# An adaLN block with dilated local attention and an MLP: two token streams in paired 64-row tiles, with Q, K and V on column tiles of the raw weights

## The chip, the cores and the metric

The kernel runs on one core of a Trainium2 chip. The metric is device time in microseconds (us) of one launch. A core has a matrix engine (TensorE, PE in the profile; its weight loads are listed as PEld), a vector engine (VectorE, DVE), an activation engine (ScalarE, ACT), a general engine (GpSimd, POOL), and a queue of its own for transfers (SyncE, SP). Each engine works through its own list of instructions in order and waits on semaphores for the others. Matmuls write into PSUM, which has eight banks; DVE and ACT read it out ("evacuate" it). TensorE's array of 128 x 128 can be used as smaller tiles: a "64x128" matmul uses 64 of its rows, and two of these, on row tiles 0 and 64, can stand in the array together; "128x32" uses 32 of its columns, and so on. Here this is called the tile mode.

## The reference

One block over 2048 tokens of width 448: a modulated layer norm, attention in which each token sees itself and seven tokens before it at a distance of 2, 4, ... 14, an output projection, a second modulated norm followed by a third norm inside the MLP, and an MLP of width 1792. Inputs and outputs are bf16.

```python
def _A_ref(x, wqkv, wo):
    B, S, D = x.shape
    H = 16
    Dh = D // H
    W, dil = (8, 2)
    qkv = (lambda x, *d: x.transpose(*d))((x @ wqkv).reshape(B, S, 3, H, Dh), 2, 0, 3, 1, 4)
    ...
    logits = jnp.where(mask[None, None, :, :], logits, -1000000000.0)
    attn = _softmax(logits, axis=-1)
    o = jnp.einsum('bhsw,bhswd->bhsd', attn, vg)
    return (lambda x, *d: x.transpose(*d))(o, 0, 2, 1, 3).reshape(B, S, D) @ wo

def _B_ref(x, w1, b1, w2, b2):
    y = _layernorm(x, axis=-1)
    h = _gelu(jnp.einsum('bsd,df->bsf', y, w1) + b1)
    return jnp.einsum('bsf,fd->bsd', h, w2) + b2
...
mod = (_silu(c) @ w_mod).reshape(c.shape[0], 6, 1, -1)
sa, ca, ga, sb, cb, gb = (mod[:, 0].copy(), mod[:, 1].copy(), mod[:, 2].copy(), mod[:, 3].copy(), mod[:, 4].copy(), mod[:, 5].copy())
h = _layernorm(x, axis=-1) * (1 + ca) + sa
x = x + ga * _A_ref(h, A_wqkv, A_wo)
h = _layernorm(x, axis=-1) * (1 + cb) + sb
x = x + gb * _B_ref(h, B_w1, B_b1, B_w2, B_b2)
```

## The kernel before

**Tokens.** With a dilation of 2, even and odd tokens never meet in the attention. So the tokens are split by parity into two streams of 1024, which lie one behind the other on the free axis (`tok_col`). A block is 128 tokens of one stream; there are 16.

**Order.** The program first records every piece of work as a task with an engine, a cost, its readers and writers and its buffers (`Planner.add`). `Planner.plan` then places the tasks in time with these costs, over several turns with noise, and `emit` writes the instructions out in the order of the best plan, with warm-up matmuls (`filler`) where PE would wait in the first 12 us. What each engine runs in which order is thus set by the planner. PSUM is divided into two double buffers (room "L", two banks each) and four single ones (room "S").

**Front.** `front_ln` takes a layer norm of some blocks (statistics L513 and L514, a reciprocal root on ACT or on POOL at L531, normalizing L536), transposes them on PE (L607) and applies the modulation in the evacuation (DVE L581, ACT L585), so that `hT` holds the normed input with the width on partitions, in four passes of 128, 128, 128 and 64 rows. `spread` (L626) copies the Q and K weights into `Wqk`, in which every head of 28 columns has 32. `front_qk` multiplies (L640): eight groups of four heads, four passes each, up to 512 tokens to a matmul, evacuated by ACT (L652) or DVE (L649). `mods` (L661) computes four of the six modulation vectors in 128x32 tiles, sends them through memory to all partitions, and folds two of them into the projection and w2 weights (L676, L685).

**Attention.** It works in nine blocks of two sub-blocks; a sub-block is two windows of 57 queries with 64 keys each. `values` copies the two windows out of `hT` (`hw`, L702) and multiplies them with the V weights (L708). The logits (L733) stand with keys on partitions, in 32x64 tiles; ACT takes the exponential (L743), DVE multiplies with the mask (L751). Then one group of matmuls sums the weights of each head (pd, L765, with a matrix of ones) and one forms the weighted values (po, L773), both in 64x32 tiles with the head's width on partitions. ACT turns the sums into reciprocals with a logarithm and an exponential (L785, L788), and DVE multiplies (L798) into `oT`, again 32 rows to a head.

**Rest.** `out_proj` (L814) projects a block of 128 tokens in four passes, and DVE adds the residual (L818); then come the second and the third norm (L829 to L836), a DMA transpose into `yT` (L840), and on POOL the residual with the MLP's bias (L844). `mlp` takes a tile of 256 tokens: w1 (L864) in 14 groups of 128 columns, four passes each, whose last pass has 64 rows and a row of ones that carries the bias b1; GELU on ACT (L871); w2 (L885) with 14 passes for each of two blocks; DVE adds (L892) and SP stores two blocks at once (L905). Exponentials and GELUs need different function tables on ACT, so the work is divided into four phases (`PHASES`): attention blocks 0 to 2 and MLP tile 0, and so on; w1 of a phase stands behind that phase's logits.

Of the kernel before, what the change touches and what calls it, by code (L numbers as in the profile page):

```python
# [11 lines left out]
FP32 = mybir.dt.float32  # L12
# [5 lines left out]
DP = 512  # L18
KT, KR = 4, 64
KW = (128, 128, 128, KR)  # L20
KE = (128, 128, 128, KR + 1)
HP = 32
FT = F // 128
WIN = 8
SL = 1024
LEAD, SEP = 8, 8
WQ, WK, WE = 57, 64, 58
SBQ, NSB, NBT = 2 * WQ, 18, 9
SBE = 4 * WE
WT = LEAD + SL + SEP + SL + 4  # L30
OTW = NSB * SBQ
NBLK = S // 128
EPS = 1e-5
DEN_SCALE = 2.0 ** -32
EXP_SET = "natural_log_exp_and_others"
START, NOISE, WINDOW = 0.8, 0.02, 3.4133
SEED, TURNS = 44, 60
QKE = "AAADAAAD"
BONUS = (0.0, 0.0, 0.0)
SPREAD = (("DVE", "DVE"), ("DVE", "DVE"))  # L40
PHASES = [
    (range(0, 3), [0]),
    (range(3, 5), [1, 2]),
    (range(5, 7), [3, 4]),
    (range(7, 9), [5, 6, 7]),
]
LMM, DMM = 0.55, 0.80
FILL_UNTIL, FILL_SHARE = 12.0, 1.0
ROOM = {"L": 2, "S": 4, "et": 2, "den": 2, "zh": 6, "yT": 3, "hm": 3, "vb": 4, "hw": 3}
SWITCH, SAME = 0.095, 1.0  # L50
SEM = 0.07
DRAIN = {"PE": 0.165, "DVE": 0.085, "ACT": 0.105, "POOL": 0.05, "SP": 0.0}


class Buf:


    def __init__(self, room, make, name=""):
        self.room, self.make, self.name, self.users, self._t = room, make, name, [], None
        self.slot = None  # L60
# [8 lines left out]
class Task:  # L69
    def __init__(self, n, eng, us, fn, bufs, rank_add, late, dense, port, mode):  # L70
        self.n, self.eng, self.us, self.fn, self.bufs = n, eng, us, fn, bufs
        self.name = f"{eng} {fn.__qualname__.split('.')[-1]}:{fn.__code__.co_firstlineno}"
        self.rank_add, self.late, self.dense, self.port, self.mode = rank_add, late, dense, port, mode
        self.before, self.after = {}, []
        self.rank = 0.0
        self.fill = 0


class Planner:

    def __init__(self):
        self.tasks, self.writer, self.readers = [], {}, {}

    def add(self, eng, us, fn, reads=(), writes=(), bufs=(), after=(), order_after=(), rank_add=0.0, late=0.0, dense=1.0, port=False, mode="F"):
        t = Task(len(self.tasks), eng, us, fn, bufs, rank_add, late, dense, port or eng == "POOL", mode)
        for k in list(reads) + [b for b in bufs]:
            if k in self.writer:
                self._edge(self.writer[k], t, True)  # L90
        for k in writes:
            if k in self.writer:
                self._edge(self.writer[k], t, True)
            for r in self.readers.get(k, ()):
                self._edge(r, t, True)
            self.writer[k], self.readers[k] = t, []
        for k in reads:
            self.readers.setdefault(k, []).append(t)
        for b in bufs:
            b.users.append(t)  # L100
        for a in after:
            self._edge(a, t, True)
        for a in order_after:
            self._edge(a, t, False)
        self.tasks.append(t)
        return t

    def wrote(self, task, *bufs):
        for b in bufs:
            self.writer[b] = task  # L110

    def _edge(self, a, b, full):
        if a is b:
            return
        if a not in b.before:
            a.after.append(b)
            b.before[a] = full
        else:
            b.before[a] = b.before[a] or full

    def ranks(self):
        for t in reversed(self.tasks):
            tail = 0.0
            for a in t.after:
                lag = (DRAIN[t.eng] + SEM + t.late) if a.before[t] else 0.0
                tail = max(tail, a.rank + lag)
            t.rank = t.us + tail + t.rank_add

    def backward(self):

        used = {e: [] for e in DRAIN}
        for t in sorted(self.tasks, key=lambda t: (-(t.start + t.us), -t.n)):
            tail = 0.0
            for a in t.after:
                same = a.eng == t.eng and (t.eng == "PE" or not a.before[t])
                lag = 0.0 if same or not a.before[t] else DRAIN[t.eng] + SEM + t.late
                tail = max(tail, a.rank + lag)
            spans = used[t.eng]
            k = bisect.bisect_left(spans, (tail, 0.0))
            if k > 0 and spans[k - 1][1] > tail:  # L140
                tail = spans[k - 1][1]
            while k < len(spans) and spans[k][0] < tail + t.us - 1e-9:
                tail = max(tail, spans[k][1])
                k += 1
            t.rank = tail + t.us
            spans.insert(k, (tail, t.rank))

    def forward(self):
        left = {t: len(t.before) for t in self.tasks}
        ready_at = {t: 0.0 for t in self.tasks}  # L150
        ready = {e: [] for e in DRAIN}
        for t in self.tasks:
            if left[t] == 0:
                ready[t.eng].append(t)
        room = {r: [0.0] * n for r, n in ROOM.items()}
        users_left = {b: len(b.users) for t in self.tasks for b in t.bufs}
        free_at = {e: START for e in DRAIN}
        order = []
        now = START
        mode = "F"  # L160
        port = {"DVE": 0.0, "POOL": 0.0}
        while len(order) < len(self.tasks):
            started = False
            for e in ("PE", "DVE", "ACT", "POOL", "SP"):
                if free_at[e] > now:
                    continue
                best, best_key = None, None
                shared = e in port and port["DVE" if e == "POOL" else "POOL"] > now
                for t in ready[e]:
                    if ready_at[t] > now or (shared and t.port):  # L170
                        continue
                    key = (t.rank + (SAME if e == "PE" and t.mode == mode else 0.0), -t.n)
                    if best is not None and key < best_key:
                        continue
                    need = {}
                    for b in t.bufs:
                        if b.slot is None:
                            need[b.room] = need.get(b.room, 0) + 1
                    if all(sum(x <= now for x in room[r]) >= n for r, n in need.items()):
                        best, best_key = t, key  # L180
                if best is None:
                    continue
                t = best
                t.fill = 0
                if e == "PE" and now < FILL_UNTIL:
                    t.fill = int(max(0.0, now - free_at[e]) * FILL_SHARE / (0.43 if now < 6.8 else 0.215))
                ready[e].remove(t)
                order.append(t)
                t.start = now
                started = True  # L190
                for b in t.bufs:
                    if b.slot is None:
                        b.slot = min(range(ROOM[b.room]), key=lambda k: room[b.room][k])
                        room[b.room][b.slot] = 1e9
                end = now + t.us
                if e == "PE" and t.mode != mode:
                    end += SWITCH
                    mode = t.mode
                free_at[e] = end
                if t.port:  # L200
                    port[e] = end
                done = end + DRAIN[e] + t.late
                for b in t.bufs:
                    users_left[b] -= 1
                    if users_left[b] == 0:
                        room[b.room][b.slot] = done + SEM
                for a in t.after:
                    left[a] -= 1
                    at = done + SEM if a.before[t] else end
                    if a.eng == e == "PE" or (a.eng == e and not a.before[t]):  # L210
                        at = end
                    ready_at[a] = max(ready_at[a], at)
                    if left[a] == 0:
                        ready[a.eng].append(a)
            if started:
                continue
            times = [v for v in free_at.values() if v > now] + [v for r in room.values() for v in r if now < v < 1e9]
            times += [ready_at[t] for e in ready for t in ready[e] if ready_at[t] > now]
            if not times:
                return None, 1e9  # L220
            now = min(times)
        return order, max(t.start + t.us + t.late for t in self.tasks)

    def clear(self):
        for t in self.tasks:
# [755 lines left out]
```

## Time and profile before

| What | us |
|---|---|
| median of 3 runs (lowest, highest) | 187.85 (187.34, 188.03) |
| span of the profiled execution, first to last instruction (the page has no other time of it) | 184.8 |
| PE busy; w1 (L864), w2 (L885), Q/K (L640) | 173.5; 52.3, 46.9, 30.0 |
| DVE busy | 124.6 |
| ACT busy; GELU (L871), exponentials (L743), denominators (L785, L788) | 103.8; 28.8, 16.0, 8.5 and 9.6 |
| POOL busy | 47.5 |
| first Q/K matmul, first w1 matmul, end of the last w2 matmul | 10.3, 54.0, 180.6 |

A line of the profile's costliest groups names the source line, the engine, the operation, what it writes and reads, the size, and how often it runs; behind the bar stand the busy time of all of them in us, the mean of one in ns, and the time for which the engine stood idle just ahead of them, with the instruction that ended it. Matmuls are pipelined, so the mean of one is longer than the distance to the next. A line of the chain in order of time has the start, the length, the engine, the tile, the line and how many instructions are merged in it; a line of the table of stretches has the stretch, its length, then the busy time and number of instructions of PE, PEld, DVE, ACT and POOL, then the granted TensorE clock as a share of full speed, the share of time in which the DMA engines were busy, and GB/s. The granted clock was 1.000 over the whole span.

### The profile page before, as it was taken

To read this page: it belongs to the slowest core of one execution; us is meant where nothing else is said; L and a number is where in the kernel's file an instruction comes from. 1 tells how busy PE (TensorE), PEld (TensorE's weight loads), DVE (VectorE), ACT (ScalarE), POOL (GpSimd) and SP (SyncE) were. 2 spreads that over 40 slices of the span, in tenths; PEclk is the share of its full clock that TensorE was granted. 3 is DMA by queue.
4 is the path that set the end of the run, shared out by engine and by line. 5 is a ranking of instruction groups with operands and counts; after the bars stand their busy time and mean duration, and the time that the engine had idled before them with its cause. 6 is when DMAs were issued, how large, how long until landed. Compare 5 with 4: busy or idle time off the path is not lost.

```text
span 184.8 us, 5433 instructions
## 1 busy us (share of the span) xinstructions
PE 173.5 (94%) x2325; PEld 111.5 (60%) x2333; DVE 124.6 (67%) x348; ACT 103.8 (56%) x139; POOL 47.5 (26%) x97
## 2 busy tenths in 40 slices
PE   3997789899999999999999999999999999999991
PEld 0574565455458655775855567678556756857750
DVE  3799599889899799688424389693346968711102
ACT  2167667767486877766585667426786530521230
POOL 7074000508501602334200060532001526200000
PEclk9999999999999999999999999999999999999999
DMA  5999779900110101301210100213001012040101
GB/s 172 304 356 265 193 175 313 326 14 7 27 32 0 28 5 32 82 0 28 42 18 0 52 5 4 57 50 48 14 4 53 0 32 78 0 103 7 51 0 50
DMA packets 19004, 13.99 MB, mean 76 GB/s; under 512 B 9246, under 2 KB 18403, under 8 KB 18980
## 3 DMA queue, kind: packets, MB, share of 16 engines
q1 hardware_dynamic: 18978, 13.64, 27.7%
q8 instruction: 18, 0.29, 0.7%
q14 instruction: 6, 0.05, 0.1%
q10 hardware_dynamic: 2, 0.00, 0.0%
HBM read 9.70 MB, written 1.84 MB: 62 GB/s over the span
## 4 chain that ended last, share of the span: by engine, by line
PE 90%; DVE 4%; issue 2%; DMA 1%; ACT 1%; DVEq 0%
PE p L864 27%; PE p L885 23%; PE pq L640 13%; PE pv L708 7%; PE pw L814 7%; PE pwm L506 3%; PE lt L733 3%; PE po L773 3%; PE ptr L607 1%; PE pd L765 1%; DMA yT<-ybuf 1%; DVE st_all L513 1%; DVE kT L649 1%; ACT lden L788 1%; PE pb L661 0%
## 5 line engine op out<-in xcount | busy, mean ns | idle before, releaser
L864 PE MATMUL p<-yT,w_s 128*128 128x256 bf16 x448 | 52.3, 272 | 0.1
L871 ACT ACTIVATE hm<-p 128x1024 bf16<-128x1024 f32 (+1 forms) x32 | 28.8, 916 | 36.8 <-PE p L864 36.8
L864 PEld LDWEIGHTS <-w_s 128*128 128x128 bf16 x448 | 43.3, 97 | 8.9 <-issue 0.6
L885 PE MATMUL p<-w_s,hm 128*128 128x448 bf16 x224 | 46.9, 353 | 0.0
L531 POOL TENSOR_TENSOR rs_all<-tv_all,neg_half 128x1 f32<-128x1 f32 (+1 forms) x35 | 20.9, 605 | 52.3 <-DVE tv_all L528 47.5
L885 PEld LDWEIGHTS <-hm 128*128 128x128 bf16 x224 | 21.2, 98 | 17.9
L844 POOL TENSOR_TENSOR x1p_ring<-x_all,gbb_bc 128x448 f32<-128x448 bf16 x16 | 17.2, 1079 | 54.6 <-DVE x_all L818 45.3
L640 PE MATMUL pq<-hT,Wqk 128*128 128x512 bf16 (+3 forms) x153 | 30.0, 334 | 0.5 <-issue 0.2
L892 DVE TENSOR_TENSOR x_all<-p,x1p_ring 128x448 bf16<-128x448 f32 x16 | 9.8, 618 | 26.0 <-PE p L885 26.0
L640 PEld LDWEIGHTS <-Wqk 128*128 128x128 bf16 (+1 forms) x160 | 15.1, 97 | 11.5 <-DVE Wqk L626 0.2
L513 DVE BATCH_NORM_STATS2 st_all<-x_all 128x6 f32<-128x448 bf16 x32 | 19.1, 617 | 0.7 <-DMA x_all<-in_A_x_dram 0.5
L743 ACT ACTIVATE et<-lt 128x928 bf16<-128x928 f32 x18 | 16.0, 941 | 5.0 <-PE lt L733 4.9
L708 PE MATMUL pv<-Wv,hw 128*128 128x448 bf16 x72 | 16.4, 353 | 1.6 <-DVE hw L702 0.9
L751 DVE TENSOR_TENSOR et<-et,mask 128x928 bf16<-128x928 bf16 x18 | 11.7, 649 | 5.3 <-ACT et L743 5.3
L814 PE MATMUL pw<-wo_s,oT 128*128 128x448 bf16 x64 | 14.4, 352 | 0.0
L712 ACT CAST vbuf<-pv 128x448 bf16<-128x448 f32 x18 | 9.6, 532 | 6.3 <-PE pv L708 6.2
L818 DVE TENSOR_TENSOR x_all<-pw,x_all 128x448 bf16<-128x448 f32 x16 | 9.9, 620 | 4.4 <-PE pw L814 4.2
L785 ACT ACTIVATE lden<-pd 128x928 f32<-128x928 f32 x9 | 8.5, 948 | 7.1 <-PE pd L765 7.1
L652 ACT CAST kT<-pq 128x512 bf16<-128x512 f32 (+1 forms) x14 | 7.1, 510 | 8.6 <-PE pq L640 8.2
L708 PEld LDWEIGHTS <-hw 128*128 128x128 bf16 x72 | 6.7, 97 | 7.7 <-issue 1.2
L798 DVE TENSOR_TENSOR oT<-po,lden 128x456 bf16<-128x456 f32 x18 | 10.6, 623 | 0.6 <-ACT lden L788 0.6
L833 DVE BATCH_NORM_STATS2 st_all<-h 128x6 f32<-128x448 bf16 x16 | 9.8, 621 | 0.1
(83 smaller groups left out, 172.3 us busy)
## 6 DMA issues: line engine op xcount, KB each, us to landing
out_dram<-x_all SPq DMA_DIRECT2D x8, 224.0 KB, 2.0
w_s<-in_B_w_dram SPq DMA_DIRECT2D x2, 784.0 KB, 12.3
wmod<-in_w_mod_dram SPq DMA_DIRECT2D x2, 672.0 KB, 7.5
w_s<-in_B_w_dram SPq DMA_DIRECT2D x1, 1344.0 KB, 9.1
x_all<-in_A_x_dram SPq DMA_DIRECT2D x1, 896.0 KB, 7.9
wm_st<-in_w_mod_dram SPq DMA_DIRECT2D x1, 720.0 KB
wqk_st<-in_A_wqkv_dram SPq DMA_DIRECT2D x2, 339.0 KB, 5.7
x_all<-in_A_x_dram SPq DMA_DIRECT2D x2, 224.0 KB
```

Of the source, the lines that this page charges most:

```text
L513: add("DVE", 0.53, lambda: nc.vector.bn_stats(out=st_all[:, sl, :], in_=src()), reads=key, writes=[f"st{sl}"])
L531: lambda: nc.gpsimd.tensor_tensor(out=rs_all[:, which, b0:b0 + n], in0=tv_all[:, which, b0:b0 + n], in1=neg_half[:, 0:n], op=ALU.pow),
L640: nc.tensor.matmul(pq.t[:], lhsT=wqk_m(kt, m), rhs=hT[0:KE[kt], kt, c0:c0 + n], start=(kt == 0), stop=(kt == KT - 1))
L708: nc.tensor.matmul(pv.t[:], lhsT=hw.t[0:KE[kt], kt].rearrange("p j k -> p (j k)"), rhs=Wv[0:KE[kt], kt, :], start=(kt == 0), stop=(kt == K ...
L743: ex = add("ACT", 0.825, lambda half=half: nc.scalar.activation(out=et.t[:, 2 * half:2 * half + 2].rearrange("p r n ft c -> p r (n ft c)") ...
L751: nc.vector.tensor_tensor(out=ev, in0=ev, in1=mask[:], op=ALU.mult)
L798: nc.vector.tensor_tensor(out=out, in0=pos[j].t[:], in1=rden.t[:, j, :, :, 0:WQ], op=ALU.mult)
L814: nc.tensor.matmul(pw.t[:], lhsT=oT[:, ft, c0:c0 + 128], rhs=wo_s[:, ft, :], start=(ft == 0), stop=(ft == 3))
L844: nc.gpsimd.tensor_tensor(out=x1p_ring[:, t % NX1P, :], in0=x_all[:, t, :], in1=gbb2_bc[:], op=ALU.add)
L864: nc.tensor.matmul(p1.t[:, f // 2, f % 2 * 256:f % 2 * 256 + 256], lhsT=w1_s[0:kp, kt, (fq + f) * 128:(fq + f + 1) * 128], rhs=yT.t[0:kp, ...
L871: gl = add("ACT", 0.18 + nf * 0.183, lambda fq=fq, nf=nf, p1=p1: nc.scalar.activation(out=hm.t[:, fq:fq + nf, :], in_=p1.t[:, 0:nf // 2, : ...
L885: nc.tensor.matmul(p2.t[:], lhsT=hm.t[:, ft, bi * 128:(bi + 1) * 128], rhs=w2_s[:, ft, :], start=(ft == 0), stop=(ft == FT - 1))
```

## The change

The kernel is written anew on the same mathematics.

- **Streams.** The two parities stand side by side: a pair p holds 128 tokens of each stream, and there are eight pairs. x is loaded and stored by pairs, with the two tokens of a row of memory together.
- **w1 and the output projection** contract over seven passes of 64 rows instead of three of 128 and one of 64. Stream 0 lies on partitions 0 to 63 and stream 1 on 64 to 127; each pass is two matmuls in 64x128 mode, one for each stream, which write different banks. The bias b1 moves into the GELU instruction. An MLP tile has 512 tokens (256 of each stream), so there are four tiles instead of eight.
- **Q, K and V** take the weights as they were loaded (`Wqkv`). Q and K: four heads at a time, each in its own 128x32 column tile, 32 raw columns from the head's first (the surplus lands in rows that are not used). V: the windows of 64 keys are read straight from `hT`, in 128x64 tiles.
- **Attention.** One batch of 114 queries of both streams, nine batches. The logits and the mask are as before. V has a 29th column of ones, so that the weighted values come with their denominators. They now stand with queries on partitions (L580, 64x64 tiles, 64 matmuls of 29 columns); DVE takes a reciprocal (L588) and multiplies (L590), and 28 matmuls with the identity (L602, 64x64 tiles) turn the result into the layout of the projection, evacuated by ACT or DVE (L609, L610). The separate sums and ACT's logarithm and exponential of them are gone.
- **PSUM** is four double buffers for everything.
- **Phases.** Three instead of four: batches 0 to 4 and tile 0, batches 5 and 6 and tile 1, batches 7 and 8 and tiles 2 and 3.
- **Loads.** The modulation weights are laid out as 4 x 112 rows, one DMA for each part; the last four pairs of x come ahead of the second part. Half of the projection weights and of w1 is issued from ACT's queue.
- **Order.** The planner is gone; the order of the tasks, the buffers they use, some choices of engine ("53:A" is task 53 on ACT) and three groups of warm-up matmuls (f3, f10, f5, in pairs) are written out as lists (`ORDER`, `SLOTS`). In this order all Q/K, seven of nine V groups, five batches of logits and values and four projections stand ahead of the first w1 matmul on PE.

The core of the diff:

```diff
+UNITS = [[0], [1], [2, 3], [4, 5], [6, 7]]
+PHASES = [(range(0, 5), [0]), (range(5, 7), [1]), (range(7, 9), [2, 3])]
+ROOM = {"P": 4, "et": 2, "os": 2, "den": 2, "z": 3, "h2": 3, "yb": 2, "yT": 2, "hm": 2, "vb": 2, "vf": 1, "xp": 3}
...
+ORDER = """
+0 2 26 9 4 10 33 24 32 11 5 1 3 12 29 13 14 15 28 f3 34 16 17 30 36 35 18 37 19 44 20 27 31 21 38 46 22 23 45 39 47 6
+40 25 7 48 8 49 51 50 f10 41 52 43 42 54 53:A 55 56:A f5 57 65 59 58 67 63 66 60 68 97 69 61 70 99 64 71 72 62 139 98
...
+    def filler(n):
+        for k in range(n):
+            for i in range(2):
+                rows = slice(KS * i, KS * i + KS)
+                nc.tensor.matmul(pwm.t[:, i, 0:512], lhsT=warm_w[rows, 0:128], rhs=warm_w[rows, :],
+                                 start=True, stop=True, tile_position=(KS * i, 0))
...
-            def mm(m=m, pq=pq):
-                for kt in range(KT):
-                    nc.tensor.matmul(pq.t[:], lhsT=wqk_m(kt, m), rhs=hT[0:KE[kt], kt, c0:c0 + n],
-                                     start=(kt == 0), stop=(kt == KT - 1))
+            def mm(m=m, pq=pq):
+                for a in range(2):
+                    for kt in range(KT):
+                        for r in range(4):
+                            w0, w = ((m + a) * 4 + r) * DH, HP if r < 3 else DH
+                            nc.tensor.matmul(pq.t[HP * r:HP * r + w, a, 0:NS * n], lhsT=Wqkv[0:KE[kt], kt, w0:w0 + w],
+                                             rhs=hT[0:KE[kt], NS * kt:NS * kt + NS, c0:c0 + n], start=(kt == 0),
+                                             stop=(kt == KT - 1), tile_position=(0, HP * r))
...
+        def vmm():
+            for kt in range(KT):
+                for j in range(2):
+                    for n in range(NS):
+                        nc.tensor.matmul(pv.t[WK * j:WK * j + WK, n, 0:D],
+                                         lhsT=hT[0:KE[kt], NS * kt + n, kc + WQ * j:kc + WQ * j + WK],
+                                         rhs=Wqkv[0:KE[kt], kt, 2 * D:3 * D], start=(kt == 0), stop=(kt == KT - 1),
+                                         tile_position=(0, WK * j))
...
+        def pmm():
+            for r in range(4):
+                for ft in range(4):
+                    h = 4 * ft + r
+                    for s in range(NS):
+                        for j in range(2):
+                            rows, col = slice(WK * j, WK * j + WK), j if s == 0 else 1 - j
+                            e0 = ((r * 2 + s) * 4 + ft) * WE
+                            nc.tensor.matmul(po.t[WK * col:WK * col + WK, s, HP * h:HP * h + DH + 1],
+                                             lhsT=et.t[rows, e0:e0 + WK], rhs=vb.t[rows, s, h, 0:DH + 1],
+                                             start=True, stop=True, tile_position=(WK * j, WK * col))
...
+        add("DVE", 0.27, lambda: nc.vector.reciprocal(out=rden.t[:], in_=heads()[:, :, :, DH]), bufs=[po, rden], fills=[rden],
+            name="rden")
+        add("DVE", 1.0, lambda: nc.vector.tensor_tensor(
+            out=osb.t[:].rearrange("p s (h e) -> p s h e", h=H), in0=heads()[:, :, :, 0:DH],
+            in1=rden.t[:].unsqueeze(3).to_broadcast([128, NS, H, DH]), op=ALU.mult),
+            bufs=[po, rden, osb], fills=[osb], name="omul")
...
+        def omm():
+            for k in range(KP):
+                for s in range(NS):
+                    for j in range(2):
+                        col = j if s == 0 else 1 - j
+                        rows = slice(WK * col, WK * col + WK)
+                        nc.tensor.matmul(pt.t[KS * s:KS * s + KS, j, k * WQ:k * WQ + WQ],
+                                         lhsT=osb.t[rows, s, k * KS:(k + 1) * KS], rhs=ident[rows, WK * col:WK * col + WQ],
+                                         start=True, stop=True, tile_position=(WK * col, KS * s))
...
-            for ft in range(4):
-                nc.tensor.matmul(pw.t[:], lhsT=oT[:, ft, c0:c0 + 128], rhs=wo_s[:, ft, :],
-                                 start=(ft == 0), stop=(ft == 3))
+            for k in range(KP):
+                for s in range(NS):
+                    rows = slice(KS * s, KS * s + KS)
+                    nc.tensor.matmul(pw.t[:, s, 0:D], lhsT=hT[rows, k, 128 * p:128 * p + 128], rhs=wo_s[rows, k, :],
+                                     start=(k == 0), stop=(k == KP - 1), tile_position=(KS * s, 0))
...
+                    for k in range(KP):
+                        for s in range(NS):
+                            rows = slice(KS * s, KS * s + KS)
+                            nc.tensor.matmul(p1.t[:, s, 256 * fi:256 * fi + 256], lhsT=w1_s[rows, k, f * 128:(f + 1) * 128],
+                                             rhs=yT.t[rows, k, :], start=(k == 0), stop=(k == KP - 1),
+                                             tile_position=(KS * s, 0))
...
+            for fi in range(2):
+                f = 2 * g + fi
+                gelus.append(add("ACT", 0.49, lambda f=f, fi=fi, p1=p1: nc.scalar.activation(
+                    out=hm.t[:, f], in_=p1.t[:, :, 256 * fi:256 * fi + 256], func=ACT.Gelu_apprx_tanh,
+                    bias=b1_col[:, f:f + 1]), reads=["b1"], bufs=[p1, hm], writes=[(hm, f)], after=[tbl], name="gelu"))
```

## The prediction

> **What bounds the kernel now.** I read the page first (busy shares, then the chain that ended last), then the table of stretches, then the chain in order of time. TensorE is the bound: it is busy for 94% of the span, and the chain runs through PE for 90% of it.
>
> ```profile
> PE 173.5 (94%) x2325; PEld 111.5 (60%) x2333; DVE 124.6 (67%) x348; ACT 103.8 (56%) x139; POOL 47.5 (26%) x97
> ...
> L864 PE MATMUL p<-yT,w_s 128*128 128x256 bf16 x448 | 52.3, 272 | 0.1
> ```
>
> L864 is the w1 product: 448 matmuls, with 0.1 us of idle time before all of them. The stretches show where PE waits (column 2 is the length, column 3 PE's busy time):
>
> ```profile
> 10.50:54.00 43.50, 39.17 (x643) 23.12 (x644) 38.94 (x110) 29.96 (x52) 14.02 (x46) 1.00 0.62 171
> 54.00:76.30 22.30, 22.19 (x407) 14.57 (x410) 20.21 (x56) 16.67 (x21) 5.03 (x8) 1.00 0.14 31
> 76.30:180.60 104.30, 104.19 (x1221) 70.21 (x1220) 57.84 (x155) 54.21 (x62) 23.77 (x33) 1.00 0.13 29
> ```
>
> From 54.0 (the first w1) to 180.6 PE never waits; before it, 4.3 of 43.5 us are idle, with DVE as busy as PE. So an instruction taken off PE is worth its spacing after 54, and before 54 the waits decide too. Spacings come from the chain in order of time (start, us, what), since a matmul's mean of 272 ns overlaps its neighbours:
>
> ```profile
> 7.97 0.78 PE ps_col L563 x32
> ...
> 18.23 0.87 PE pb L661 x16
> ...
> 30.69 3.47 PE pq L640 x16
> ...
> 64.25 0.63 PE lt L733 x64
> ...
> 67.64 0.63 PE lt L733 x63
> 68.28 0.86 PE p L885 x4
> ...
> 87.59 6.17 PE p L864 x56
> ...
> 106.28 1.51 PE pw L814 x8
> ...
> 108.55 0.32 PE pd L765 x8
> 108.87 0.55 PE po L773 x64
> ```
>
> Read here: w1 costs 6.17/56 = 0.110 us for 256 columns, the output projection 1.51/8 = 0.189 for 448, Q/K 3.47/16 = 0.217 for 512. Four w2 matmuls take 0.76 elsewhere in the chain but 0.86 behind a logits group in another tile mode, so one mode change costs 0.10. The pd row carries eight matmuls of 464 columns on 2 row tiles by 4 column tiles: one after the other they would take 8 x 0.19 = 1.5 us, and they take 0.32. Tiles of the array do run side by side, in both directions. The pb row says it for 128x32 tiles alone: 16 matmuls of 448 columns in 0.87, four rounds of 0.19 and a mode change.
>
> **The sum, against the span of 184.8.**
>
> *w1 in row pairs.* 448 matmuls become 784, two streams in row tiles 0 and 64, each pair writing two banks, as pd did. At one spacing per pair: 392 x 0.110 = 43.2 instead of 49.4: -6.2. The seventh half-filled contraction pass (64 rows and a bias row) is what disappears. *Output projection:* 64 x 0.189 = 12.1 becomes 56 pairs, 10.6: -1.5. w2 stays at 224.
>
> *Mode changes.* Counting the places where the PE order changes tile mode: 39 before, 60 after, 21 x 0.10 = +2.1.
>
> *Q/K on raw columns.* 160 matmuls become 640 in 128x32 mode, four to a round, 160 rounds of the same columns. Bounds: nothing (pb's 0.87 is 0.76 and one mode change), or the whole surplus of pb, (0.87 - 0.76)/4 = 0.028 a round, +4.4. I take +0.5, near the lower end, because the mode change explains nearly all of it. V, in two 128x64 column tiles, keeps 72 rounds; bounds 0 and 72 x 0.028 = 2.0, taken as 0 on the same row.
>
> *Attention.* Before: pd and po, 0.87 a block, 0.77 without the mode change. After: 64 matmuls in 64x64 tiles and 28 that turn the result back. At po's 0.55/64 = 8.6 ns each, 0.55 + 0.24 = 0.79: +0.2 over nine blocks. At logits' 0.63/64 = 9.8 ns they make 0.90, +1.2. No row has four 64x64 tiles; the far end is a rival below. I take po's price, the nearest shape.
>
> *Start.* Before its 32 column matmuls PE runs 7 warm-up matmuls at 3.07/7 = 0.44 us; the new order puts 10 pairs there, +1.3 if they are as slow. Against it the spreading copies of the Q/K weights go (DVE, 9.90 to 10.78, just ahead of the first Q/K at 10.51), worth up to 0.3. I take +0.7, so Q/K starts at 11.2. The four evacuations of the first unit keep their prices (0.73 for two on DVE, 1.02 for two on ACT).
>
> *End.* Before, two adds (1.15 us together) and a 224 KB store stand behind the last matmul; after, one add (0.62) and half that store: -0.6.
>
> *Other engines.* ACT loses the logarithm and exponential of the denominators (9 x 0.948 + 9 x 1.069 = 18.1) and gains about 4 in smaller GELUs (56 x 0.595 against 24 x 1.024 + 8 x 0.595) and some 4 in evacuations of the turned output. DVE loses 1.8 of spreading and 5.4 of window copies, and its 18 divisions (10.6) become nine of double width (L818's 0.62 for 448 columns gives about 1.1, an estimate: 9.8) with nine reciprocals (some 0.2 each). All counted as nothing: from the first w1 on both have slack (58 and 54 us busy of 104). Without that cover a w2 evacuation of 1.1 us would stop PE eight times, +9.
>
> *Waits.* w1 now stands behind five attention blocks instead of three, all Q/K and seven of nine V groups. PE's work up to there: Q/K 28.4, V 7 x 1.51 = 10.6, logits and values 5 x (0.53 + 0.79) = 6.6, projection 5.3, transposes 3.2 (seven of 0.45), modulation 0.9, 36 mode changes 3.6: 58.6, so w1 could begin at 69.8. DVE's list up to the second y of the first pair, at the spacings of the chain and timeline (statistics 0.53, normalizing 0.31, mask 0.55), comes to 53 us from about 5: it ends 11 us sooner if never held up, where before its slack was 43.5 - 38.9 = 4.6. The wait on window copies (0.9 us of PE idle) goes. I lower idle time, 5.1 before by the same sums, by 1.1. *DMA:* the six-vector modulation weights now come behind 1.2 times the bytes (5.4 against 4.5 MB, which were in by about 18), so near 21.5 at that rate, and part of the projection weights rides on ACT's queue from the start. Their matmuls (L481) stand in PE's order at about 24; were they late, every Q/K behind them would wait, and then the scale rows and the w1 and w2 loads behind those on SP's queue. The DMA transposes go from 16 to 8 with seven blocks instead of four; 2.4 us to landing now, up to 7/4 of it then, behind which only w1 of a later pair stands, with other PE work ahead.
>
> Sum: -6.2 - 1.5 + 2.1 + 0.5 + 0.2 + 0.7 - 0.6 - 1.1 = -5.9, span 178.9. The runs' median, 187.85, is 3.05 above the profiled span; the page gives no other time of that execution, and I keep the difference: **181.9 us**.
>
> **Rivals.**
>
> *1. The 64x64 matmuls take turns (slower).* In po and pt both row tiles write the same bank, on different partitions. Before, pd, po and the logits gave each row tile a bank of its own, so no row shows it. If the two row tiles alternate, 0.79 becomes 1.58 a block, +7.1: 189.0. It decides from +6.9 on (187.85 + 0.5%). For it: the overlap that pd's 0.32 shows is with a bank for each. Against: the partitions differ.
> The Trainium skill (TensorEngine Tiling, Restrictions and Gotchas, Gotcha 1) says that different row tiles can't access one bank at the same time; no run here shows it yet, and by that rule this rival is the result.
>
> *2. Weight loads come into the open in the column tiles.* ps_col is nearly all weight loads: 0.78/32 = 24 ns each. Four a round on 160 rounds, if none were hidden, +15.6: 197.5. Against it: pb, whose 16 loads leave nothing to see.
> The Trainium skill (TensorEngine Tiling, Restrictions) says column tiling switches Fast Weight Load off; pb's 0.87 gives no sign of a cost.
>
> *3. Row pairs don't overlap.* Then w1 is 784 x 0.110 and the projection 112 x 0.189: +53.8, 235.7. pd's 0.32 speaks against it.
>
> *4. The first stage starves.* All products now share four two-bank buffers where two double and four single ones stood, and all engines follow one fixed list. If PE idles as it did from 10.5 to 30 (3.2 of 19.5 us) over all of its 58.6 us, that is 11.6 instead of 4.0: +7.6, 189.5; half of it 185.7. For it: DVE was as busy as PE there. Against: DVE's slack of 11 us.
>
> **How the numbers follow.** Forecast 0.68 (own range 177 to 186), rival 1 0.11, rival 2 0.06, rival 3 0.03, rival 4 0.12. The lower end, 176.5, is the forecast with Q/K at nothing (-0.5), the start at its other bound (-1.0) and none of the 4.0 us of idle time left; the upper, 190, takes in rivals 1 and 4; rivals 2 and 3 and scraps, about a tenth, are left out. About 0.5% is what runs of this kernel can tell from no change (their spread is 0.4%): 186.9 to 188.8. Faster: 0.66 of the forecast and 0.02 of rival 4. Same: 0.02 of the forecast, 0.02 of rival 1 (half paid), 0.03 of rival 4. Slower: the rest, 0.25.
>
> **What would show it.** 28 w1 matmuls (one group of L675) in 1.54 us of chain; the projection's 14 in 1.33; 32 Q/K of 512 in 1.74; L580 0.55 and L602 0.24 a block (twice that is rival 1); first Q/K near 11.2, first w1 near 74; no PE idle time behind it. A first w1 beyond 80, or PE waiting for DVE after it, would make the prediction wrong.

## The result and the profile after

The changed kernel is slower: 198.03 us (median of 4 runs, 196.81 to 199.34) against 187.94 for the kernel before on the same chip, a ratio of 1.0575 with a 95% interval of 1.0471 to 1.0679. The forecast was 181.9 with a range of 176.5 to 190.0, so it was wrong in direction and in range. The profiled execution took 196.81 us, with a span of 195.0 (forecast: 178.9). Of most of these programs some executions are a few per cent slower, at a lower granted clock; the ratios below compare the others, and the traces of e1 and e10 come from such slow executions.

The page of the changed kernel, the same rows as before: the engines' busy time, the w1 group, then the granted clock in the 40 slices and two rows on DMA.

```profile
PE 173.0 (89%) x3463; PEld 111.0 (57%) x3463; DVE 117.7 (60%) x272; ACT 93.7 (48%) x128; POOL 40.1 (21%) x71
...
PEclk9999879998569999999999999999999999999998
...
q8 instruction: 27, 0.44, 1.0%
...
HBM read 11.70 MB, written 1.84 MB: 69 GB/s over the span
...
L675 PE MATMUL p<-yT,w_s 64*128 64x256 bf16 x784 | 44.3, 269 | 0.4 <-issue 0.4
```

TensorE is as long busy as before (173.0 against 173.5), and w1 runs almost without idle time, as forecast. But PE's share fell from 94% to 89%, and the clock drops twice, around 25 and around 52 us. The queue q8 brings instructions: 27 pieces of 16 KB, where the page before has these rows:

```profile
q8 instruction: 18, 0.29, 0.7%
...
HBM read 9.70 MB, written 1.84 MB: 62 GB/s over the span
```

The stretches say where the time is. First the two parts that the first w1 matmul (89.58) divides, then the first part in six pieces; columns as in the table before (PE's busy time is the third, the clock the one after the last engine, then the DMA share).

```profile
9.92:89.58 79.66, 63.17 (x1665) 38.20 (x1667) 55.20 (x129) 39.31 (x50) 12.95 (x16) 0.91 0.48 129
89.58:191.69 102.11, 101.38 (x1720) 69.16 (x1716) 57.09 (x126) 51.83 (x73) 22.07 (x24) 1.00 0.13 33
```

```profile
10.00:23.00 13.00, 8.77 (x269) 6.97 (x270) 9.75 (x31) 7.37 (x13) 1.48 (x2) 1.00 1.06 306
23.00:26.50 3.50, 3.49 (x55) 2.65 (x56) 2.17 (x8) 1.12 (x2) 0.00 (x0) 0.51 0.44 91
26.50:43.00 16.50, 14.68 (x441) 9.00 (x439) 11.58 (x26) 8.83 (x12) 3.72 (x5) 1.00 0.49 114
43.00:47.00 4.00, 2.79 (x144) 1.97 (x141) 3.55 (x9) 3.01 (x5) 0.00 (x0) 1.00 1.06 375
47.00:57.20 10.20, 4.26 (x40) 2.32 (x43) 2.69 (x4) 3.29 (x5) 0.00 (x0) 0.50 0.76 195
57.20:89.58 32.38, 29.10 (x728) 15.21 (x722) 25.37 (x54) 15.69 (x17) 7.75 (x9) 1.00 0.09 17
```

The second part is as forecast: 102.1 us, where the sum had 101.5 (178.9, less 73.8 for the first w1 and 3.6 for the tail). The whole miss lies before the first w1, which came at 89.6 instead of 73.8. PE was idle there for 16.5 us instead of 4.0, and from 47.0 to 57.2 it worked for 4.26 us in 10.2, at half clock, while DVE was busy for only 2.7 us, ACT for 3.3 and POOL not at all. The chain in order of time shows what it waited for (start, length, what; "issue" is a wait with no releaser):

```profile
19.80 1.48 PE pq L458 x36
21.28 1.73 issue
23.01 2.92 PE pq L458 x51
...
44.27 0.23 PE po L580 x8
44.50 1.21 issue
45.72 0.62 PE po L580 x56
46.34 0.63 PE lt L553 x60
46.97 0.92 PE ptr L428 x8
47.89 5.94 issue
53.83 1.03 PE ptr L428 x8
54.87 3.02 PE pq L458 x28
57.89 0.61 PE po L580 x64
...
76.41 1.84 PE pq L458 x32
...
82.58 0.57 PE pt L602 x56
...
89.58 10.70 PE p L675 x196
...
149.19 1.32 PE pw L622 x14
```

The first two cut a group of like matmuls in two: in the list of PE's instructions the first falls 13 matmuls into a group of 32, after one matmul of a round of four, and the second between 8 and 56 of 64 weighted values. No data can be missing there. The third stands between the transposes of two pairs; the second pair's input had been normalized on VectorE at 45.0, 2.9 us before the wait began. What fails to come is the instructions themselves. Counting TensorE's rows in the trace (weight loads, matmuls, semaphores) from its first, the three waits begin after 705, 1729 and 1985 rows, each of them 193 + 256 k. The two waits without releaser in the trace before are at rows 449 and 961, the same series, and they too split a group:

```profile
19.41 0.12 PE po L773 x18
19.53 1.29 issue
20.82 0.49 PE po L773 x42
...
34.47 0.52 PE po L773 x61
35.00 0.70 issue
35.70 0.20 PE po L773 x3
```

So PE's program arrives in pieces of 256 instructions, by the DMA engines, and PE stands where a piece ends and the next has not landed.

### The profile page after: what moved, and what is told of

It is laid out like the page before. It is cut to its first block, busy times and chain, and to the rows that moved or that the text cites. A ratio compares the mean times of both kernels' runs of the same rounds, so it can differ in the third digit from the quotient of the medians.

```text
span 195.0 us, 7547 instructions
## 1 busy us (share of the span) xinstructions
PE 173.0 (89%) x3463; PEld 111.0 (57%) x3463; DVE 117.7 (60%) x272; ACT 93.7 (48%) x128; POOL 40.1 (21%) x71
## 3 DMA queue, kind: packets, MB, share of 16 engines
HBM read 11.70 MB, written 1.84 MB: 69 GB/s over the span
## 4 chain that ended last, share of the span: by engine, by line
PE 74%; DMA 10%; issue 5%; DVE 4%; ACT 4%; ACTq 0%; DVEq 0%
PE p L694 22%; PE p L675 21%; PE pq L458 10%; PE pv L531 8%; PE pw L622 6%; DMA wo_s<-in_A_wo_dram 4%; DMA Wqkv<-in_A_wqkv_dram 3%; PE po L580 3%; DMA mod_bc<-mod_hbm 3%; DVE hT L610 2%; PE lt L553 2%; ACT hT L439 2%; DVE wo_s L495 1%; ACT hT L609 1%; PE pt L602 1%
## 5 line engine op out<-in xcount | busy, mean ns | idle before, releaser
L683 ACT ACTIVATE hm<-p,b_col 128x512 bf16<-128x512 f32 x56 | 35.6, 684 | 31.0 <-PE p L675 30.8
L675 PE MATMUL p<-yT,w_s 64*128 64x256 bf16 x784 | 44.3, 269 | 0.4 <-issue 0.4
L675 PEld LDWEIGHTS <-w_s 64*128 64x128 bf16 x784 | 37.8, 94 | 6.3 <-issue 1.0
L458 PE MATMUL pq<-hT,Wqkv 128*32 128x512 bf16 (+7 forms) x640 | 32.7, 357 | 4.0 <-ACT hT L439 2.1
L399 POOL TENSOR_TENSOR rs_all<-tv_all,neg_half 128x2 f32<-128x2 f32 x22 | 17.0, 782 | 87.4 <-DVE tv_all L397 84.5
L458 PEld LDWEIGHTS <-Wqkv 128*32 128x32 bf16 (+3 forms) x640 | 17.9, 101 | 16.5 <-issue 7.0
L383 DVE BATCH_NORM_STATS2 stt<-x_all 128x6 f32<-128x448 bf16 x32 | 18.6, 609 | 1.8 <-DMA x_all<-in_A_x_dram 1.7
L659 POOL TENSOR_TENSOR Wqkv<-x_all,gbb_bc 128x448 f32<-128x448 bf16 x12 | 12.9, 1097 | 32.6 <-DVE x_all L704 17.7
L531 PE MATMUL pv<-Wqkv,hT 128*64 128x448 bf16 (+1 forms) x144 | 15.3, 359 | 2.2 <-DMA Wqkv<-in_A_wqkv_dram 1.1
L622 PE MATMUL pw<-wo_s,hT 64*128 64x448 bf16 x112 | 11.6, 350 | 3.6 <-ACT hT L609 2.3
```

What stands on the lines that cost most here:

```text
L383: add("DVE", 0.53, lambda: nc.vector.bn_stats(out=stt[:, w, b, :], in_=src()), reads=reads, bufs=bufs, writes=[f"st{w}_{b}"], name="stats")
L399: add("POOL", 0.42 + 0.15 * n, lambda: nc.gpsimd.tensor_tensor(out=r, in0=tv, in1=neg_half[:, 0:n], op=ALU.pow), reads=[f"tv{w}_{b0}", "ne ...
L458: nc.tensor.matmul(pq.t[HP * r:HP * r + w, a, 0:NS * n], lhsT=Wqkv[0:KE[kt], kt, w0:w0 + w], rhs=hT[0:KE[kt], NS * kt:NS * kt + NS, c0:c0 ...
L531: nc.tensor.matmul(pv.t[WK * j:WK * j + WK, n, 0:D], lhsT=hT[0:KE[kt], NS * kt + n, kc + WQ * j:kc + WQ * j + WK], rhs=Wqkv[0:KE[kt], kt, ...
L622: nc.tensor.matmul(pw.t[:, s, 0:D], lhsT=hT[rows, k, 128 * p:128 * p + 128], rhs=wo_s[rows, k, :], start=(k == 0), stop=(k == KP - 1), til ...
L659: add("POOL", 1.0, lambda n=n: nc.gpsimd.tensor_tensor(out=x1p.t[:, n, :], in0=xn(p, n), in1=gbb2_bc[:], op=ALU.add), reads=[f"x{p}", "gbb ...
```

## The experiments

Three theories at first. A: the pieces of PE's program stand in the DMA engines behind the bulk loads. B: the half of the projection weights on ScalarE's queue delays the loads behind it. C: VectorE's list is held at the scaling that waits for the modulation rows. Each run has its own runs of the kernel before beside it (medians 186.3 to 187.1).

**Fewer bytes (e1_small_w).** Only a seventh of w1 and w2 is loaded, and the products use that seventh again and again; all instructions stay.

```diff
-                load_half(eng, i, w1_s[:, :, cols], B_w1[:, cols], ...)
+                load_half(eng, i, w1_s[:, 0:1, cols], B_w1[0:KS, cols], ...)
...
-   lhsT=w1_s[rows, k, f * 128:(f + 1) * 128]
+   lhsT=w1_s[rows, 0, f * 128:(f + 1) * 128]
```

> Of the w1 and w2 weights only one seventh is loaded (and used for all passes), so the product isn't the MLP's; every instruction of every engine stays. Theory A (TensorE's instructions, fetched by DMA in pieces of 16 KB, stand behind the 3.1 MB of w1 and w2): the two waits without a releaser at 44.5 and 47.9 us (1.21 and 5.94) go, and the stretch at half clock from 47 to 57 with them; the 1.73 us at 21.3 stays; first w1 at about 80 instead of 89.6, ratio to the kernel before 1.00 (0.99 to 1.01). Theory B (half of the projection weights on ScalarE's queue delays the loads behind it) and theory C (the projection's scaling waits for the modulation rows at 38.7 and holds VectorE's list): nothing in front of these waits changes, ratio 1.04 to 1.06.

Measured: ratio 1.0031 [0.9973, 1.0090]. The waits at rows 1729 and 1985 are gone; the one at row 705 stays (4.07 us at 23.98), where x and the other weights are still loading. Of PE's waits, these two have no releaser:

```profile
PE pq L458 <- issue: 4.1, 1, 4.1
...
PE pv L531 <- issue: 0.3, 1, 0.3
```

In this trace the first w1 is at 86.2 and not near 80: its first Q/K came 3.6 us later than in the changed kernel's trace, and the wait at row 705 was 2.3 us longer. With the same instructions, some 4 MB less to load brings the ratio from 1.0575 to 1.0031, about 10 us: A, and neither B nor C, which this edit leaves as they were.

**The projection's half on SP (e2_wo_sp)**, and **with w1 and w2 right behind it (e3_early_w).**

```diff
-    load_half("ACT", 1, wo_s, A_wo, "wo", 9.0)
+    load_half("SP", 1, wo_s, A_wo, "wo", 9.0)
```

> The half of the projection weights that was issued from ScalarE's queue at 1.4 us goes to SyncE's queue, behind the other half. Theory B: the V weights' issue no longer waits until 9.67, the first V begins at 14.2 instead of 15.25 and the six-vector modulation weights land about 4 us sooner; if that is what the first stage lacked, first w1 moves by 3 to 5 us and the ratio is 1.03. Theory A: only the 1.1 us ahead of V is won; the wait of some 6 us near 48 stays; ratio 1.045 to 1.06.

> As e2, and the w1 and w2 loads stand on SyncE's queue right behind the projection weights, ahead of the modulation's round trip, which was ahead of them. Theory A: all bulk data is in by about 33 us, no wait without a releaser over 1.3 us after that, but one or two of 1.5 to 4 us between 13 and 33, where the loads now follow each other without a gap; first w1 75 to 80, ratio 0.985 to 1.01. Theory C: the modulation rows land at 38.7 or later as before, and the 6 us near 48 stay; ratio 1.03 to 1.06.

Measured: 1.0613 [1.0552, 1.0674] and 1.0675 [1.0604, 1.0747]. B falls: the order of that load wins nothing, and the long wait stays (6.58 us). The forecast that A gave for e3, 0.985 to 1.01, is missed by far. There the 6 us wait is gone from its place, but row 961 now waits 2.1 us under the earlier loads, and the modulation rows stand behind w1 and w2 (their copy to all partitions starts at 44.5 instead of 33.8), which holds PE for 3.6 us through VectorE. So the loads hurt here too, only at another place among the short matmuls.

**Small pieces, one at a time (e4_paced).** w1 and w2 in 12 transfers of some 0.4 MB, each let go by a one-element copy on GpSimd behind some evacuation; e2's edit is in it.

> All of w1 and w2 is loaded, in twelve pieces of about 0.4 MB instead of six of 0.8 MB, each let go by one element that POOL copies when a later step of the first stage (an evacuation of Q/K, hT or the turned output) is done; the projection weights are both on SyncE's queue; the scaling of w2 stands a little later in VectorE's list. Theory A (instruction pieces wait behind queued bulk data): after 34 us at most some 1 us of data is queued at any time, so no wait without a releaser over 1.3 us there and no half clock from 47 on; the one of 2 us near 21 stays; first w1 77 to 82, ratio 0.98 to 1.01. Theory C (the scaling of the projection weights behind the modulation rows): nothing changes in it, ratio 1.04 to 1.06.

Measured: 1.0625 [1.0556, 1.0693]; row 1985 still waits 3.79 us. A in the form "a long queue of bulk loads" is too simple. The piece for that row started 3.2 us late instead of 5.7: some of the 12 transfers kept the DMA engines full just then. What counts is whether the DMA engines are full when a piece is asked for.

**Fewer instructions (e5_full_qk).** Q and K go back to full-array matmuls on spread weights, 160 instead of 640; the bytes stay. The operand of the warm-up matmuls moves into w2's space to make room for the spread weights.

```diff
-                        for r in range(4):
-                            w0, w = ((m + a) * 4 + r) * DH, HP if r < 3 else DH
-                            nc.tensor.matmul(pq.t[HP * r:HP * r + w, a, 0:NS * n], ... tile_position=(0, HP * r))
+                        w = Wqk[0:KE[kt], kt, (m + a) // 4, (m + a) % 4 * 4:(m + a) % 4 * 4 + 4, :]
+                        nc.tensor.matmul(pq.t[:, a, 0:NS * n], lhsT=w.rearrange("p r e -> p (r e)"), ...)
```

> One part of the change undone: Q and K in full-array mode on weights spread to 32 columns a head (two copies on VectorE, two on ScalarE), 160 matmuls instead of 640; loads as in the changed kernel. The same rounds of columns, 960 instructions fewer on TensorE. Theory A in its full form (too many instructions, fetched behind bulk data): 4 pieces fewer to fetch, all in the loads' time, and the three waits of 8.9 us shrink to 4 or less; ratio 1.00 to 1.03. Theory A in its short form (bulk data alone decides, a piece is late whenever it is asked for behind w1 and w2): the wait near 48 stays at 4 to 6 us, ratio 1.04 to 1.06.

Measured: 1.0232 [1.0177, 1.0288], median 191.0, 23 pieces instead of 27, first w1 at 83.4. The chain of this run keeps two such waits:

```profile
40.77 1.59 issue
...
48.00 2.21 issue
```

They are at rows 1217 and 1473, other places of the program and again 193 + 256 k: the place follows the count of instructions, not the work. Together with e4's pacing (e6_both) it gave no more.

> e4 and e5 together. Theory A: fewer pieces and none behind a long queue: no wait without a releaser over 1.3 us, first w1 74 to 78, ratio 0.96 to 0.99. If the first stage lacks something else (theory C, or VectorE's list), first w1 stays beyond 82 and the ratio above 1.01.

Measured: 1.0249 [1.0180, 1.0318], with one wait of 3.0 us at row 1473 and the first w1 at 83.6. This misses A's range and falls where the expectation put something else that the first stage lacks: waits for evacuations of 6.9 us are left ahead of the first w1, beside that wait and 6.8 us at half clock.

**Loads behind the dense stretch (e7_late_w), and that with full-array Q and K (e8_late_full).** One gate in place of twelve: the four loads of w1 and the two of w2 start on SP when unit [6, 7] is transposed, and w2's scaling stands later on DVE.

```diff
+    add("POOL", 0.1, lambda: nc.gpsimd.tensor_copy(out=w1_s[0:1, 0, 0:1], in_=hT[0:1, 4, LEAD + 768:LEAD + 769]), name="gate")
+    add("SP", 0.3, lambda: nc.sync.dma_start(out=dst, in_=src), name="load late")
```

> All of w1 and w2 is loaded on SyncE's queue only after the transposes of the fourth unit (a one-element copy on GpSimd reads their result and lets the queue go), and the scaling of w2 stands later on VectorE's list; nothing else differs from the changed kernel. In the changed kernel's trace TensorE's waits without a releaser all begin in the middle of a group of like matmuls, and the number of TensorE rows before them is 193 + 256 k (705, 1729, 1985): the end of a 16 KB piece of its instructions. The next piece starts to move 3.7 to 5.7 us after the piece before it was begun when the DMA engines are full, and within 1.8 us when they are idle. Theory A (pieces stand behind bulk loads): rows 1729 and 1985 now come while the loads are not yet under way, so the waits of 1.2 and 5.9 us at 44.5 and 47.9 go, with the 10.2 us at half clock behind them (about 5 us); a piece during the loads (row 2241 or 2497) may be late by up to 3 us. Ratio to the kernel before about 1.00 to 1.025, first w1 at 77 to 83. Rival (the short matmuls use up instructions faster than they can be fetched even with idle DMA engines): a wait of 2 us or more stays at row 1985, ratio 1.04 or more. Rival (the weights come too late now): TensorE waits ahead of the first w1 for a load.

> The late loads of the run beside it together with Q and K in full-array matmuls on spread weights (160 matmuls instead of 640, with the spreading copies of the kernel before). The run with full-array Q and K alone had waits of 1.8 and 2.4 us at rows 1217 and 1473 (again 193 + 256 k) and twice 3.4 us at half clock, at 1.023 of the kernel before. Theory A: both waits fall into the time before the loads and go, with the half clock: 191.0 - 4.2 - 3.4 = 183.4, and up to 3 us for a piece that is late during the loads: ratio 0.98 to 1.00, first w1 at 75 to 79. Rival (the waits have another cause in this part of the program): ratio 1.02 as without the late loads.

Measured: 1.0337 [1.0224, 1.0450] and 0.9960 [0.9910, 1.0009]. In e7 rows 1729 and 1985 run without a wait; a new one of 1.51 us is at row 3009, under the moved loads, and row 705 still waits for 3.25. Its ratio lies between those of theory and rival; the wait at row 705 was 1.5 us longer than in the changed kernel's trace, under loads that this edit doesn't touch. e8 has neither early wait, and the clock stays full. Its stretches and its last wait:

```profile
9.92:78.81 68.89, 59.06 (x1185) 34.68 (x1187) 54.50 (x126) 40.44 (x52) 13.69 (x17) 1.00 0.60 148
78.81:180.70 101.89, 101.30 (x1721) 69.33 (x1716) 59.97 (x132) 51.77 (x73) 22.71 (x24) 1.00 0.13 33
```

```profile
65.96 0.99 PE po L585 x107
66.96 1.36 issue
68.32 0.36 PE po L585 x21
```

PE is busy for 59.06 us before its first w1, where the forecast had 58.6, and first w1 comes at 78.8.

The pieces of several traces side by side (worked out from the DMA records of q8 and the count of rows; "begun" is when the first row of the piece before it ran, "full" a DMA share of 1.0 or more in between):

```
kernel  row    piece before begun  this piece starts  late by  DMA    row runs   wait
before   449        14.21              18.18            3.98   full     20.82     1.3
before   961        28.38              32.93            4.55   full     35.70     0.7
after    449        10.75              12.57            1.81   full     16.41   none
after    705        16.41              20.10            3.69   full     23.01     1.7
after   1217        28.87              29.70            0.83   idle     35.23     none
after   1729        39.45              43.30            3.85   full     45.71     1.2
after   1985        45.71              51.42            5.71   full     53.83     5.9
after   2497        58.51              59.83            1.32   idle     67.89     none
e1      1985        49.11              48.51           -0.60   idle     51.34     none
e5      1473        42.36              47.86            5.50   full     50.20     2.2
e7      1985        44.13              43.48           -0.66   idle     46.37     none
e7      3009        66.75              70.17            3.42   full     72.68     1.5
e8      2241        62.63              65.92            3.30   full     68.32     1.4
```

A piece starts about when the one before it is begun, never two pieces ahead. With idle DMA engines it starts within 1.3 us of that here, and within 1.6 in all traces. With full ones it starts 3.3 to 5.7 us later in these rows (6.1 at most, in e3), but not always: row 449 of the changed kernel was 1.8 us late and held nothing up. In all these waits PE goes on 2.3 to 2.9 us after the start. Where a piece held PE up, its instructions thus came some 6 to 8 us after those before them were begun. In the changed kernel, rows 1729 to 1985 (weighted values, logits, half the transposes) took 2.2 us to run.

From the first Q/K matmul to the first w1, the traces compare like this (us; sums of PE's waits and of the granted clock's stretches at half speed):

| kernel | waits for instructions | other waits | PE busy | at half clock |
|---|---|---|---|---|
| changed | 8.9 | 7.6 | 63.0 | 13.7 |
| e1, fewer bytes | 4.4 | 7.1 | 61.0 | 3.6 |
| e5, fewer instructions | 3.8 | 5.9 | 62.2 | 6.8 |
| e7, late loads | 5.3 | 6.9 | 61.5 | 3.4 |
| e8, both | 1.4 | 7.3 | 58.9 | 0 |

The edits act on the waits for instructions and on the half clock, while the other waits stay at 6 to 8 us.

**Two attempts on what is left.** e8 waits mostly for evacuations. In e9 the first two w1 groups stand ahead of the last projections; in e10 the transposes of b1 and the scaling of w2 move behind what they hold up.

> The late loads with full-array Q and K, and two changes of the lists: the first two groups of w1 stand ahead of the last two projections on TensorE, and the scaling of w2 stands behind the projections' evacuations on VectorE. In the run without these changes the transposed input of the first MLP tile has landed at 74.1, but TensorE waits 1.75 us at 74.1 for the evacuations ahead of the last two projections and begins w1 at 78.8. Theory (what is left is waits of the fixed lists ahead of the first w1): the first w1 starts near 74.5, and the wait for the evacuations goes, partly back as waits later: 1 to 2.5 us less than 185.5, ratio to the kernel before 0.980 to 0.992. Rival (the evacuations or the load of w1 only come later and hold w1 or the projections instead): ratio 0.996 or more.

> The late loads with full-array Q and K, and two other changes of the lists, each at a wait that its trace shows: the transposes of b1, which hold TensorE 1.3 us at 24.5 for a load, stand behind the modulation matmuls, and the scaling of w2 stands behind the evacuations of the last two batches on VectorE, where two of them (2.0 us) hold the evacuation that the last projections wait for. Theory (what is left are such waits of the fixed lists): first w1 near 76, ratio to the kernel before 0.975 to 0.99. Rival (each wait is taken over by the next one late, as w1 ahead of the projections only moved its wait): ratio 0.993 or more, the same waits under other names.

Measured: 0.9885 [0.9804, 0.9966] and 0.9895 [0.9839, 0.9952]. e9's first w1 is at 75.1, but its PE is busy for as long as e8's from 74 to 92 (16.24 and 16.25 us of 18): the wait only moved, to the residual and an evacuation on VectorE (0.9 us each), as the rival said. In e10 the first w1 is at 81.0, not near 76; the wait for b1 is gone, but the one ahead of the last projections stays at 1.7 us: the evacuation waits for the last Q/K matmuls, since the output is written into `hT`, which these still read. Both ratios lie where the theory put them, but neither trace bears its mechanism out, and the intervals of e8, e9 and e10 overlap, so what each list change is worth stays open. e10's profiled run can't tell more: its first modulation weights held PE for 2.3 us at the start. By its ratio, e10 is about 1% faster than the kernel before.

## Why the prediction was wrong

*Right, by the rows of the chain.* The w1 tile took 10.70 us for 98 pairs, 0.109 a pair (0.110 forecast); 14 projection matmuls 1.32 to 1.50 (1.33); 32 Q/K of 512 columns 1.84 (1.74); after the first w1 102.1 us (101.5). The start was better than forecast (first Q/K at 9.92, not 11.2). The 3.05 us between span and time came out by luck: every run here lies about 1.7 us above its own span (the profiled one 196.81 above 195.0), and the median is 3.0 above that span only because the profiled run was the fastest of the four.

*Attention: the term slightly low.* A po group measured 0.61 and half of a pt pair 0.285, mode changes included, against 0.55 and 0.24.

*Rivals 1 to 3 are out.* Rival 1 needed 1.1 us for a po group; 0.61 is close to the price with overlap. The Trainium skill (TensorEngine Tiling (Array Packing), Restrictions and Gotchas, Gotcha 1) says that different row tiles can't access one bank at the same time. The po group can't decide this: at the projection's 0.189 us for 448 columns, its 64 matmuls of 29 columns would need an estimated 0.39 us if only two ran at a time, less than the 0.61 measured. The pt group can: 28 matmuls of 57 columns would need an estimated 0.34 us that way, and took 0.285 each in the pair at 82.58, mode change included. So the rule doesn't show in this form, where two row tiles write different partitions of one bank. Rival 2's open weight loads would have made 32 Q/K of 512 columns about 0.8 us longer than 1.74; they took 1.84. Rival 3 fails by w1's 10.70.

*The step that failed is "Waits".* It lowered PE's idle time ahead of the first w1 from 5.1 to 4.0; it was 16.5. That is +12.5 of the 15.8 us by which the first w1 was late. Of the 16.5, 8.9 are the three waits for instructions, and about 7.6 are waits for ACT, DVE and one load (projections 3.3, Q/K 2.1, V 2.2). The remaining +3.3 are PE's own work, 63.2 us instead of 58.6, less the better start of 1.3: 7.75 us of that work ran at half clock, which is worth up to 3.9 (half of it).

Three things in the view before could have warned me, and the prediction used none. The chain before shows two waits without a releaser, which I added into the idle time without asking what they are. The Q/K term priced 480 more matmuls by their columns alone; with as many weight loads they are nearly four of the nine pieces that PE gained, and all lie ahead of the first w1. And the DMA paragraph counted the bytes ahead of the modulation weights, but not that w1 and the projection weights are now loaded once for each stream: HBM read rises by 2.0 MB, 1.6 of them w1, and these loads fall on the densest matmuls.

*Rival 4 had the place right* (PE starves in the first stage, chance 0.12), with a cause that explains only part: buffers and lists account for the 7.6 us above, within the 4.0 to 11.6 it reached for; full-array Q and K with late loads, which leave those lists almost as they were, bring the ratio from 1.0575 to 0.9960, 11.6 us. Up to the first w1 the traces give nearly that: 7.5 us less of waits for instructions and 4.1 us less of PE's work, against 1.0 us lost by a later first Q/K. So instruction supply, with the half clock behind it, was about 12 us of the 16 us miss, as far as e8's spreading copies and its moved scaling of w2 cost nothing.

In the changed kernel a piece that came late held PE for up to 5.94 us. The Trainium skill (Runtime: NRT & Kernel Launch, Instruction fetch mechanics) says that an engine's program is refilled in blocks of 16 KiB or 256 instructions, the next page being fetched while the current one runs, and that crossing a boundary is mostly hidden because instructions are issued more slowly than they are fetched. The sizes agree with the trace; "hidden" does not where short matmuls meet full DMA engines.

## What to carry to other kernels

Count instructions as well as columns: four small tiles in place of one matmul cost nothing on the array, but four times the program to fetch, in pieces of 256 that share the DMA engines with the loads. A wait without a releaser that splits a group of like matmuls is a missing piece; its remedies are fewer instructions there, or bulk loads that start later. The two worked better together (0.996) than either alone (1.034, 1.023).

## What the runs showed of the hardware

- PE's instruction pieces, as above: up to 5.7 us late behind full DMA engines. Even with nearly idle ones (a share of 0.25) there was a short wait: in the changed kernel the 256 rows of two groups of weighted values began at 112.4, and PE waited 0.4 us at row 4545, until 2.7 us after the next piece had started.
- Behind waits like these the granted clock went to 0.5, for 3.4 us or a multiple of it: 3.4 and 10.2 us in the changed kernel, 10.2 twice in e2, none in e8 up to its last matmul, where the longest such wait was 1.4 us. A wait of 1.77 us for an evacuation, at 84.99 in the changed kernel, had none behind it, so the length of a single wait doesn't settle it. At half clock eight transposes took 0.92 to 1.03 us; 28 Q/K matmuls took 3.02, while 32 took 1.84 at full clock. That the waits cause it was not tried by itself.
- 128x32 column tiles, four to a round, ran at the price of one full-array matmul: 32 of 512 columns in 1.84 us in the changed kernel's chain, and eight full-array ones in 1.84 in e8's.
